# An attention and gMLP kernel on one core: the output product of batches five and six as seven block products

## The chip, the core and the metric

The kernel runs on one core of a Trainium2 chip. Its time is the device time of one execution in microseconds (us), given as the median of several runs. Names of engines here: TensorE (PE in rows, PEld where it loads weights), VectorE (DVE), ScalarE (ACT), GpSimd (POOL), and SyncE (SP), which here issues every DMA.

## What is computed

The input is q, k and v for 8 batches of 8 heads with 576 positions of 64 channels, and the weights of one gated layer. All of it is float32.

```
q_s = softmax(q, over the 64 channels);  k_s = softmax(k, over the 576 positions)
x   = heads joined( q_s @ (k_s^T @ v) )                 # per batch 576 x 512
h   = gelu(x @ w_in)                                     # 512 -> 1024
u, v = the two halves of h
v_n = layernorm(v) * g_ln
v_s = w_sg @ v_n + b_sg                                  # 576 x 576 over positions
out = x + (u * v_s) @ w_out                              # 512 -> 512
```

The last line's product is the one that is changed, in two of the eight batches.

## The kernel before

Batches are numbered 0 to 7. Everything of a batch lies with channels on the 128 partitions and the 576 positions along a row, so that a 512-channel matrix is four row blocks of 128. Each large product is made in float32 precision from three products of a reduced format: an operand z is stored as a high part (a cast, on ScalarE) and a low part (z minus its high part, on VectorE or GpSimd), and high*high, high*low and low*high are summed in PSUM.

The steps of a batch, by the names that stand in the code:

- `kv_all` multiplies exp(k) with v, and `x_mm` multiplies that by q; `x_kv` (L708) issues both, `x_mm` of one batch and `kv_all` of the next. `x_get` and `x_tail` (ScalarE) copy x from PSUM to `xf`, of which there are two, for even and odd batches.
- `hv_mm` makes the v half of h, 128 positions at a time (12 matmuls of 512 columns); `hv_gelu`, `hv_sq` or `hv_stat`, `hv_norm`, `hv_high` and `hv_low` follow, and leave the normed v in the two tiles `vnh` and `vnl`.
- The u half of h is computed from batch 2 on by seven block products, as Strassen's method in Winograd's form has it: `us_mm` 1 to 7 (L913), 12 matmuls of 128x288 each, on sums of blocks of x (`d_add`, `d_high`, `d_low`) and of w_in (the `sw_` steps, made once). `us_one` and `us_add` (L945) gather the blocks from three PSUM tiles, `us_gelu` follows.
- `sg_mm` is the product with w_sg, 28 matmuls of 128x288 for each of four 128-channel blocks d; `gate` multiplies by u in place, `gate_high` (L975) and `gate_low` (L978) split the product.
- `out_mm` (L990) is the output product: for each of four blocks e of 128 output channels 24 matmuls of 128x288 (four blocks d, three pairs of parts, two column halves). `out_add` (L993) adds it to x in `xf` on VectorE, `out_store` (L997) writes 288 KB to memory. In the last batch the fourth block goes by `last_mm`, in three pieces.

PSUM has three tiles of two banks (`ps2`), which products take in rotation, and two of one bank (`ps1`) for `hv_mm` and `kv_all`. The order of all work is a string of step names, PLAN, that is read once from front to back: each engine's queue, and SyncE's queue of DMAs, is in the order in which PLAN names the steps, and an engine runs its own queue strictly in that order. Semaphores between engines follow from which tile a step reads and writes; a tile with a tag of its own has a fixed home in SBUF, and a new tile in the same home waits until all users of the one before are through.

All matmuls are issued by the helper at L246, all work of the other engines by the helper at L160 of the class InOrder, so in the profile lines tell little and tiles tell what a row is.

Of the kernel before, what the change touches and what calls it, by code (L numbers as in the profile page):

```python
# [51 lines left out]
hv_norm 0 0, load_kt 2 2, q_mul 1 1 0, q_turn 1 2, kv_mm 1 0, kv_inv 1 0, hv_stat 0 0 A, kv_scale 1 0, kv_mm 1 1, kv_inv 1 1, load_w_sg 0, ws_h 0
hv_sq 0 2, hv_stat 0 2 A, kv_scale 1 1, load_q 2 0, load_kt 2 3, kt_max 2 3, x_mm 1, x_get 1 1, kt_max 2 2, load_q 2 1, ws_l 0, x_tail 1, q_max 2 0
hv_pow 0 2, load_v 2 0, hv_pow 0 0, load_b, x_endh 1, load_kt 3 0, hv_norm 0 3, x_sum 1, x_endl 1, hv_norm 0 2, load_w_sg 4, x_get 1 0, hv_mm 0 1
x_high 1 0, x_low 1 0, x_high 1 1, x_low 1 1, hv_gelu 0 1, hv_pow 0 3, hv_high 0 3, hv_low 0 3, hv_high 0 2, hv_low 0 2, hv_high 0 0, hv_stat 0 1
hv_mm 0 4, load_k 2 0, hv_norm 0 1, hv_pow 0 1, x_ownh 1, kt_put 2, ws_h 4 V, hv_gelu 0 4, hv_stat 0 4, hv_mm 1 1, hv_gelu 1 1 A, hv_sq 1 1
hv_high 0 1, load_v 2 1, hv_norm 0 4, hv_low 0 1, ws_l 2 V, hv_low 0 0, hv_mm 1 0, q_max 2 1, hv_pow 0 4, kt_max 3 0, tail_high 0, tail_low 0
tail_again 0, b_h, b_l, ws_l 4 V, hv_gelu 1 0 A, hv_mm 1 3, sg_mm 0 1, tail_high 1, load_w_out 0, load_k 2 1, kt_get 2, wo_a 0, hv_sq 1 0, sg_mm 0 0
k_sub 2 0, load_kt 3 2, hv_gelu 1 3, q_swapm 2 0, k_sub 2 1, wo_b 2, k_exp 2 0, load_kt 3 1, k_exp 2 1, wo_b 0, wo_d 2, q_swapm 2 1 G, q_top 2 1
wo_h 2, wo_d 0, wo_h 0, sg_mm 0 3, gate 0 0, gate_high 0 0, gate 0 1, hv_mm 1 2, gate_high 0 1, kt_max 3 1, q_sub 2 1, kt_max 3 2, tail_low 1  # L60
q_top 2 0, wo_l 0 V, q_sub 2 0, gate 0 3, load_kt 3 3, kt_max 3 3, kt_put 3, kt_get 3, q_exp 2 1, q_sum 2 1, sg_mm 0 2, wo_l 2 V, hv_gelu 1 2 A
hv_sq 1 2, kv_all 2, gate 0 2, q_exp 2 0, gate_high 0 2, load_k 3 1, q_swapd 2 1, load_k 3 0, gate_low 0 0, gate_high 0 3, gate_low 0 1, gate_low 0 2
gate_low 0 3 G, hv_stat 1 0 A, q_sum 2 0, q_inv 2 1, load_v 3 0, kv_inv 2 0, kv_scale 2 0, out_mm 0 0, out_add 0 0, kv_inv 2 1, q_swapd 2 0 G
q_inv 2 0, kv_scale 2 1, hv_stat 1 3, q_mul 2 0 0 V, q_mul 2 1 1, tail_again 1, q_turn 2 3, out_mm 0 3, out_add 0 3, q_mul 2 0 1, q_turn 2 1
q_mul 2 1 0, q_turn 2 2, k_sub 3 1 G, k_exp 3 1, q_turn 2 0, out_mm 0 1, load_kt 4 0, out_add 0 1, load_v 3 1, k_sub 3 0, out_mm 0 2, out_add 0 2
x_ownl 1, out_store 0 1, sw_get 1 1, k_exp 3 0, x_kv 2, hv_norm 1 1, hv_stat 1 1 A, out_store 0 0, x_get 2 0, hv_norm 1 3, sw_get 1 0, out_store 0 2
sw_add 1, sw_high 1, out_store 0 3, kt_max 4 0, x_tail 2, x_get 2 1, sw_get 0 0, hv_pow 1 3, hu_mm 1 2, sw_add 3, hu_gelu 1 2, hv_stat 1 2 A, sw_add 2
sw_high 2, hu_mm 1 0, hu_gelu 1 0, load_kt 4 1, kt_max 4 1, hu_mm 1 3, kv_inv 3 0, kv_scale 3 0, hv_pow 1 0, hv_pow 1 1, hv_high 1 1, kv_inv 3 1
sw_get 0 1, sw_add 4, load_k 4 1, kv_scale 3 1, sw_low 1, load_v 4 0, load_kt 4 2, kt_max 4 2, load_kt 4 3, kt_max 4 3, kt_put 4, hv_norm 1 0
hv_high 1 0, hv_norm 1 2, hv_low 1 0, sw_high 3, hv_pow 1 2, hv_low 1 1, hv_high 1 2, sw_low 2, sw_low 3, load_kt 5 0, kt_get 4, hv_high 1 3  # L70
hv_low 1 2, sw_high 4, sw_low 4, hv_low 1 3, load_q 3 0, hu_gelu 1 3, kt_max 5 0, hu_mm 1 1, x_high 2 0, x_high 2 1, sg_mm 1 0, q_max 3 0, q_swapm 3 0
# [1014 lines left out]
```

## Time and profile before

| | |
|---|---|
| median of 3 runs | 481.65 us (481.62, 481.65, 483.18) |
| the profiled execution's own time | 482.25 us |
| its span, first to last instruction | 480.4 us |
| TensorE busy | 474.9 us (99%) |
| TensorE loading weights | 437.7 us (91%) |
| VectorE busy | 372.8 us (78%) |
| ScalarE busy | 272.8 us (57%) |
| GpSimd busy | 141.8 us (30%) |

The busy time of TensorE is modelled, since its matmuls overlap each other: one matmul of 128x288 lasts 0.29 us in a row, and the next one begins after 0.13 us. The pace is therefore read from the times at which matmuls start. The granted clock of TensorE is 1.00 in every stretch that is shown, which is the level of 2.4 GHz. The rows that matter stand below, ahead of the prediction.

### The profile page before, as it was taken

To read this page: it belongs to the slowest core of one execution; us is meant where nothing else is said; L and a number is where in the kernel's file an instruction comes from. 1 tells how busy PE (TensorE), PEld (TensorE's weight loads), DVE (VectorE), ACT (ScalarE), POOL (GpSimd) and SP (SyncE) were. 2 spreads that over 40 slices of the span, in tenths; PEclk is the share of its full clock that TensorE was granted. 3 is DMA by queue.
4 is the path that set the end of the run, shared out by engine and by line. 5 is a ranking of instruction groups with operands and counts; after the bars stand their busy time and mean duration, and the time that the engine had idled before them with its cause. 6 is when DMAs were issued, how large, how long until landed. Compare 5 with 4: busy or idle time off the path is not lost.

```text
span 480.4 us, 9342 instructions
## 1 busy us (share of the span) xinstructions
PE 474.9 (99%) x3813; PEld 437.7 (91%) x3813; DVE 372.8 (78%) x604; ACT 272.8 (57%) x439; POOL 141.8 (30%) x157
## 2 busy tenths in 40 slices
...
GB/s 307 367 407 200 297 187 69 192 210 191 242 47 53 124 175 138 49 155 159 154 0 1 157 144 89 132 26 124 51 1 27 75 0 1 1 0 76 0 1 124
DMA packets 20637, 57.11 MB, mean 119 GB/s; under 512 B 3057, under 2 KB 3569, under 8 KB 20594
## 3 DMA queue, kind: packets, MB, share of 16 engines
...
## 4 chain that ended last, share of the span: by engine, by line
PE 90%; DVE 4%; ACT 2%; DMA 2%; issue 1%; POOL 0%; POOLq 0%
PE ps L246 90%; DMA qq<-q 1%; DMA kmt<-kt 1%; DVE xf L160 1%; DVE qqw L160 1%; DVE wi_l L160 0%; ACT qs L160 0%; DVE ktall L160 0%; DVE v L160 0%; ACT qq L160 0%; ACT vnh L160 0%; DVE qm L160 0%; ACT x_l L160 0%; ACT xf L160 0%; DVE wi_h L160 0%
## 5 line engine op out<-in xcount | busy, mean ns | idle before, releaser
L160 DVE TENSOR_TENSOR u<-ps,u 128x576 f32<-128x576 f32 x62 | 46.3, 753 | 35.7 <-PE ps L246 32.9
L160 POOL TENSOR_TENSOR rs<-ve,half 128x1 f32<-128x1 f32 x36 | 27.8, 779 | 116.3 <-DVE ve L160 115.2
L246 PE MATMUL ps<-gh,wo_h 128*128 128x288 f32 (+1 forms) x260 | 56.5, 295 | 0.0
L246 PE MATMUL ps<-gh,wo_l 128*128 128x288 f32 (+1 forms) x260 | 56.2, 293 | 0.0
L246 PE MATMUL ps<-ws_h,vnh 128*128 128x288 f32 x256 | 55.0, 296 | 0.4 <-ACT u L160 0.4
L246 PE MATMUL ps<-ws_l,vnh 128*128 128x288 f32 x256 | 54.8, 295 | 0.0
L246 PE MATMUL ps<-ws_h,vnl 128*128 128x288 f32 x256 | 54.8, 295 | 0.0
L160 ACT ACTIVATE v<-ps 128x512 f32<-128x512 f32 x36 | 21.4, 596 | 39.3 <-PE ps L246 39.0
L160 ACT ACT_TABLE_LOAD x30 | 38.5, 1283 | 8.4 <-PE ps L246 4.0
L246 PEld LDWEIGHTS ps<-gh,wo_h 128*128 128x128 f32 x260 | 42.3, 189 | 0.7
L246 PEld LDWEIGHTS ps<-ws_h,vnh 128*128 128x128 f32 x256 | 41.5, 188 | 1.1 <-ACT u L160 0.6
L246 PEld LDWEIGHTS ps<-gh,wo_l 128*128 128x128 f32 x260 | 42.2, 188 | 0.0
L246 PEld LDWEIGHTS ps<-ws_l,vnh 128*128 128x128 f32 x256 | 41.3, 188 | 0.0
L246 PEld LDWEIGHTS ps<-ws_h,vnl 128*128 128x128 f32 x256 | 41.3, 188 | 0.0
L246 PE MATMUL ps<-wi_l,x_h 128*128 128x512 f32 x144 | 39.6, 396 | 0.2 <-DVE wi_l L160 0.2
L246 PE MATMUL ps<-wi_h,x_h 128*128 128x512 f32 x144 | 39.6, 397 | 0.1
L160 DVE TENSOR_TENSOR xf<-ps,xf 128x576 f32<-128x576 f32 (+2 forms) x34 | 24.0, 714 | 20.2 <-PE ps L246 20.1
L246 PE MATMUL ps<-wi_h,x_l 128*128 128x512 f32 x144 | 39.6, 396 | 0.0
L160 ACT CAST gh<-u 128x576 fp32r<-128x576 f32 x32 | 21.0, 670 | 25.5 <-DVE u L160 24.8
L246 PEld LDWEIGHTS ps<-wi_l,x_h 128*128 128x128 f32 x144 | 27.0, 188 | 7.1 <-DVE wi_l L160 0.6
L246 PEld LDWEIGHTS ps<-wi_h,x_l 128*128 128x128 f32 x144 | 27.0, 188 | 6.9 <-DVE x_l L160 0.5
L160 ACT ACTIVATE vnh<-v,rs 128x512 fp32r<-128x512 f32 x32 | 22.2, 719 | 17.5 <-DVE v L160 13.8
...
## 6 DMA issues: line engine op xcount, KB each, us to landing
...
out<-xf SPq DMA_DIRECT2D x31, 288.0 KB, 2.1
...
kmt<-kt SPq DMA_DIRECT2D x24, 288.0 KB, 3.0
...
ghws<-w_sg SPq DMA_DIRECT2D x5, 288.0 KB, 8.2
```

Of the source, the lines that this page charges most:

```text
L160: ins = op(*args, **kw)
L246: tc.keep_in_program_order(nc.tensor.matmul(*args, **kw))
```

## The change

In batches 5 and 6 (`SEVEN = range(5, B - 1)`) the steps `out_mm`, `out_add` and `out_store` are gone. In their place stand seven block products `os_mm` 1 to 7 of 12 matmuls each, on 2x2 blocks of the gated product (128 x 2 x 288) and of w_out (128 x 2 x 256).

- Once: `so_get` (4) adds high and low parts of a block of w_out, `so_add` (4) makes the four sums that the method needs, `so_high` and `so_low` (4 each) split them. They lie in the homes of k (`kk`), v (`vv`) and the transposed k (`km`), which are free once batch 7 has used them.
- For each of the two batches: `e_add` (4) makes sums of blocks of the gated product in place, `e_high` and `e_low` (4 each) split them, into `vnh` and `vnl` and a half of the first gated tile; nine `os_add` gather the result from three PSUM tiles into `xf`; four `os_store` write it. Of the first two blocks d `gate_high` and `gate_low` split only the first 288 columns there, and the low part of the last two lies in a home of v.
- From `hv_gelu 0 3` on, PLAN is a new string: the same steps otherwise, in another order, in batches 0 to 7.

The diff without PLAN:

```diff
+SEVEN = range(5, B - 1)
...
     def gate_rest(b, d):
         if d < 2:
-            return sd_all()[:, 12 * DH + d * S:12 * DH + d * S + S]
+            return low_one()[:, d]
+        if b in SEVEN:
+            return vv_s("low", b, at=1, shape=[P, 2, S], dt=F32R)[:, d - 2]
         return uu_s("low", b, at=0, dt=F32R)[:, d - 2]
+    def used(b, d):
+        return slice(0, HS if b in SEVEN and d < 2 else S)
...
+    def o_block(i, j):
+        hi, lo = wo_hl()
+        return block(hi, i, j, DH), block(lo, i, j, DH)
+
+    def o_parts(n):
+        if n == 3:
+            return [km_s("so", t, at=1 - t, dt=F32R)[:, 0:2 * DH].rearrange("p (c n) -> p c n", c=2) for t in range(2)]
+        z = (vv_s if n == 4 else kk_s)("so", n, at=n - 1 if n < 3 else 0, shape=[P, 2, 2, DH], dt=F32R)
+        return [z[:, t] for t in range(2)]
...
+    def so_get(i, j, E=V):
+        hi, lo = o_block(i, j)
+        E.tensor_tensor(out=o_whole(i, j), in0=f32(hi), in1=f32(lo), op=ALU.add)
...
+        a, b, op = {
+            1: (o_whole(1, 0), o_whole(1, 1), ALU.add), 2: (o_whole(1, 1), o_whole(0, 0), ALU.subtract),
+            3: (o_whole(0, 0), o_whole(1, 0), ALU.subtract), 4: (o_whole(0, 1), o_whole(1, 1), ALU.subtract),
+        }[n]
...
+    def e_parts(b, n):
+        if n == 1:
+            return [gh_s(b, 0, at=0)[:, :, HS:S], low_one()[:, :, HS:S]]
+        k, z = 2 * n - 4, [y.rearrange("p a n -> p (a n)") for y in vn_hl()]
+        return [z[m // 3][:, m % 3 * S:m % 3 * S + S].rearrange("p (c n) -> p c n", c=2) for m in (k, k + 1)]
+
+    def e_sum(b, n):
+        return u_block(b, *{1: (0, 0), 2: (1, 1), 3: (0, 1), 4: (1, 0)}[n])
+
+    def e_add(b, n, E=V):
+        x, y = {1: ((0, 1), (0, 0)), 3: ((1, 1), (0, 1)), 2: ((1, 1), (0, 0)), 4: ((1, 0), (1, 1))}[n]
+        E.tensor_tensor(out=e_sum(b, n), in0=u_block(b, *x), in1=u_block(b, *y), op=ALU.subtract)
...
+    def os_mm(b, n, fresh=0):
+        l, r, name = {
+            1: (o_block(0, 0), lambda: g_block(b, 0, 0), "oa"), 2: (o_block(0, 1), lambda: g_block(b, 1, 0), "oa"),
+            3: (o_parts(4), lambda: g_block(b, 1, 1), "oc"), 4: (o_block(1, 1), lambda: e_parts(b, 4), "ob"),
+            5: (o_parts(1), lambda: e_parts(b, 1), "oc"), 6: (o_parts(2), lambda: e_parts(b, 2), "ob"),
+            7: (o_parts(3), lambda: e_parts(b, 3), "ob"),
+        }[n]
...
+        for s in range(2):
+            fs, m = slice(s * P, s * P + P), 0
+            for p, q in ((0, 0), (1, 0), (0, 1)):
+                for c in range(2):
+                    mm(st[name, b][:, s, 0:HS], l[p][:, c, fs], r[q][:, c], start=bool(fresh) and m == 0, stop=m == 5, skip_group_check=not fresh)
+                    m += 1
...
+    def os_add(b, k, i, j):
+        o = xf(b)[:, 2 * i:2 * i + 2, j * HS:j * HS + HS]
+        V.tensor_tensor(out=o, in0=us_sum(b, banks[k]), in1=o, op=ALU.add)
+
+    def os_store(b, i, j):
+        js = slice(j * HS, j * HS + HS)
+        to = out[b, 2 * i * P:(2 * i + 2) * P, js].rearrange("(c p) n -> p c n", c=2)
+        Y.dma_start(out=to, in_=xf(b)[:, 2 * i:2 * i + 2, js])
```

What the new order does is shown at three places, in the queues of the engines. The helpers' lines are L160 and L246 before, L166 and L252 after; the digits in a tile's name are the batch and the block, and a number of the allocation.

**First place: ScalarE's queue in batch 1.** Here `u1_..<-ps2` is `hu_gelu 1` (the gelu of one 128-channel block of u, which frees a PSUM tile), and `qs3_0<-qm3_0` is `q_swapm 3 0`, which waits for a maximum over a q tile that a DMA has to bring. Before:

```order
L160 ACTIVATE u1_1_1378<-ps2_0_80 128x576
L160 CAST x_h_74<-xf0_76 128x2x576 x2
L160 COPY qs3_0_1548<-qm3_0_1546 32x36 x4
L160 ACTIVATE u1_0_1408<-ps2_1_81 128x576
L160 ACT_TABLE_LOAD
```

and with the change:

```order
L166 ACTIVATE u1_0_1371<-ps2_0_80 128x576
L166 CAST wi_h_61<-qqw_1_1279 128x2x256
L166 CAST x_h_74<-xf0_76 128x2x576
L166 CAST sd_1112<-qqw_1_1279 128x512
L166 ACTIVATE u1_1_1428<-ps2_1_81 128x576
L166 COPY qs3_0_1583<-qm3_0_1576 32x36 x4
```

The last gelu of batch 1's u stands ahead of the copies that wait for the q tile; before it stood behind them.

**Second place: ScalarE's queue behind `x_kv 6`.** `xf0<-ps2` are `x_get 6 0`, `x_get 6 1` and (128x2x2x64) `x_tail 6`; `ghd` are high parts for `us_mm`; `u5_1<-ps2` is `us_one 5`. Before:

```order
L160 CAST ghd_5_2_3746<-ud_5_0_3722 128x576
L160 CAST sd_1117<-ud_5_1_3604 128x576
L160 COPY xf0_76<-ps2_1_81 128x2x512
L160 COPY xf0_76<-ps2_2_82 128x2x512
L160 ACTIVATE vnh_607<-v5_0_3554,rs5_0_3689 128x512
L160 COPY xf0_76<-ps2_0_80 128x2x2x64
L160 COPY u5_1_3868<-ps2_1_81 128x2x288
```

and with the change, where `kkso_1` is `so_high 1`, whose home is that of batch 7's k:

```order
L166 ACTIVATE vnh_586<-v5_2_3506,rs5_2_3596 128x512
L166 ACTIVATE vnh_586<-v5_3_3626,rs5_3_3672 128x512
L166 COPY xf0_76<-ps2_1_81 128x2x512
L166 CAST kkso_1_3849<-kmso_1_1_3541 128x512
L166 CAST ghd_5_2_3859<-ud_5_0_3757 128x576
L166 COPY xf0_76<-ps2_2_82 128x2x512
L166 CAST ghd_5_4_3867<-ud_5_0_3757 128x576
L166 COPY u5_1_3881<-ps2_1_81 128x2x288
L166 COPY xf0_76<-ps2_2_82 128x2x2x64
```

Two splits and a cast of a w_out sum now stand between the three copies that free PSUM; the cast waits for the last read of k by `kv_all 7`.

**Third place: TensorE's queue at the end of batch 5's output product.** `gh5`, `ulow_5` are the gated product's parts, `wo_h` and `wo_l` those of w_out, `vnh`, `vnl` here the parts of the e sums, `qt7` and `kvt7` the operands of `x_mm 7`. Before, the end of `out_mm 5 2`, `hv_mm 6 2`, and the start of `x_mm 7`:

```order
L246 MATMUL ps2_2_82<-gh5_1_4083,wo_l_961 128x288 x2
L246 MATMUL ps1_1_84<-wi_h_61,x_h_74 128x512 x4
L246 MATMUL ps1_1_84<-wi_h_61,x_l_75 128x512 x4
L246 MATMUL ps1_1_84<-wi_l_62,x_h_74 128x512 x4
L246 MATMUL ps2_0_80<-qt7_0_4137,kvt7_0_4014 64x512
```

and with the change, the end of `os_mm 5 2`, `os_mm 5 4`, and `x_mm 7`:

```order
L252 MATMUL ps2_2_82<-vvlow_5_4168,wo_h_951 128x288 x2
L252 MATMUL ps2_0_80<-vnl_587,wo_h_951 128x288 x2
L252 MATMUL ps2_0_80<-vnl_587,wo_l_952 128x288 x2
L252 MATMUL ps2_0_80<-vnl_587,wo_h_951 128x288 x4
L252 MATMUL ps2_0_80<-vnl_587,wo_l_952 128x288 x2
L252 MATMUL ps2_0_80<-vnl_587,wo_h_951 128x288 x2
L252 MATMUL ps2_2_82<-qt7_0_4028,kvt7_0_4106 64x512
L252 MATMUL ps2_2_82<-qt7_0_4028,kvt7_1_4095 64x512
L252 MATMUL ps2_2_82<-qt7_0_4028,kvt7_0_4106 64x512
L252 MATMUL ps2_2_82<-qt7_0_4028,kvt7_1_4095 64x512
L252 MATMUL ps2_0_80<-qt7_1_4171,kvt7_0_4106 64x512
```

No `hv_mm` stands between the output product and `x_mm 7` any more, and the second half of `x_mm 7` takes the PSUM tile `ps2_0` that the last block product has just filled. The three `hv_mm` of batch 6 (for positions 0, 3 and 2 of the blocks of 128) stand ahead of `os_mm 5 6` instead.

## Rows read from the trace of the kernel before

**Rows 1.** The page: span, and busy time of each engine.

```profile
span 480.4 us, 9342 instructions
PE 474.9 (99%) x3813; PEld 437.7 (91%) x3813; DVE 372.8 (78%) x604; ACT 272.8 (57%) x439; POOL 141.8 (30%) x157
```

**Rows 2.** Chain that ended last: start us, us, what; its last long pieces, from a DMA on.

```profile
119.21 5.02 DMA qq<-q
...
126.57 0.66 ACT u L160
...
127.27 350.32 PE ps L246 x2720
```

**Rows 3.** TensorE's timeline: start us, us of the merged row, shapes, count, idle before.

```profile
71.76 1.04 PE L246 MATMUL ps<-ws,vn 128*128 128x288 f32 x4
...
126.19 0.70 PE L246 MATMUL ps<-ws,vn 128*128 128x288 f32 x4
127.27 0.53 PE L246 MATMUL ps<-ws_h,vnh 128*128 128x288 f32 x2 [0.38 <-ACT u L160]
```

**Rows 4.** TensorE's timeline at an output product: an `out_mm`, an `hv_mm`, the next `out_mm`.

```profile
309.73 0.43 PE L246 MATMUL ps<-gh,wo_h 128*128 128x288 f32 x2
...
312.89 1.09 PE L246 MATMUL ps<-wi_h,x_h 128*128 128x512 f32 x4
...
315.68 0.43 PE L246 MATMUL ps<-gh,wo_h 128*128 128x288 f32 x2
```

**Rows 5.** TensorE's timeline from `x_mm` and `kv_all` on to block products `us_mm`.

```profile
328.10 2.18 PE L246 MATMUL ps<-qt,kvt 64*64 64x512 f32 x32
330.10 2.43 PE L246 MATMUL ps<-vv,kk 64*64 64x65 f32 x80
332.46 0.53 PE L246 MATMUL ps<-x_h,wi_h 128*128 128x288 f32 x2
...
334.17 1.75 PE L246 MATMUL ps<-ghd,sd 128*128 128x288 f32 x12
335.75 1.76 PE L246 MATMUL ps<-sd 128*128 128x288 f32 x12
```

**Rows 6.** Costliest groups by form: shapes, count | busy us, mean ns | idle before, releaser.

```profile
L160 DVE TENSOR_TENSOR xf<-ps,xf 128x576 f32<-128x576 f32 x31 | 23.0, 748 | 14.8 <-PE ps L246 14.8
L160 ACT COPY xf<-ps 128x1024 f32<-128x1024 f32 x14 | 13.9, 1016 | 4.3 <-PE ps L246 2.4 <-DMA out<-xf 1.9
L160 DVE TENSOR_TENSOR qqw<-wi_h,wi_l 128x512 f32<-128x512 f32 x4 | 2.7, 680 | 0.0
L160 ACT CAST sd<-qqw 128x512 fp32r<-128x512 f32 x3 | 1.8, 611 | 2.4 <-DVE qqw L160 2.4
L160 ACT CAST sd<-ud 128x576 fp32r<-128x576 f32 x6 | 4.0, 670 | 1.3 <-PE ps L246 1.3
```

**Rows 7.** VectorE's timeline: two splits of the same form, one behind the other.

```profile
329.39 0.76 DVE L160 TENSOR_TENSOR ghd<-ud,ghd 128x576 fp32r<-128x576 f32 x1 [0.92 <-ACT ghd L160]
330.07 0.76 DVE L160 TENSOR_TENSOR sd<-ud,sd 128x576 fp32r<-128x576 f32 x1
```

**Rows 8.** Stretches: from:to, us; busy (x) of PE, PEld, DVE, ACT, POOL; clock, DMA.

```profile
60.00:120.00 60.00, 59.89 (x552) 55.77 (x551) 57.10 (x97) 40.57 (x67) 28.89 (x22) 1.00 0.52 170
271.24:328.58 57.34, 57.34 (x469) 53.11 (x464) 46.03 (x74) 33.22 (x49) 9.32 (x16) 1.00 0.33 107
328.58:380.34 51.76, 51.76 (x445) 48.63 (x440) 37.91 (x62) 26.52 (x48) 11.73 (x13) 1.00 0.13 46
```

**Rows 9.** DMA issues: KB each, median us to landing; then least, median, longest.

```profile
out<-xf SPq DMA_DIRECT2D x31, 288.0 KB, 2.1
DMA to landing us min/median/max: 1.6/2.1/5.0
```

**Rows 10.** The tile `sd`: splits on VectorE and GpSimd, ns least/median/longest.

```profile
L160 DVE TENSOR_TENSOR sd<-u,gh x9: 749/753/1368, 87.6 to 460.8; 128x576 fp32r<-128x576 f32 x9
L160 POOL TENSOR_TENSOR sd<-u,gh x7: 1422/1435/2267, 141.6 to 461.7; 128x576 fp32r<-128x576 f32 x7
```

More of the change, by code (lines that the diff above doesn't have):

```diff
@@ L52 @@
[L52 to L71, printed above, removed]
@@ new lines @@
+so_low 1, out_store 4 2, d_add 5 4, d_high 5 2, x_get 6 1, so_get 0 0, kv_inv 7 0, d_low 5 2, d_high 5 4, us_mm 5 1, us_one 5, so_add 2, d_low 5 4
+x_tail 6, x_high 6 0, so_add 3, us_mm 5 5, us_add 5 5, q_inv 7 0, hv_pow 5 1, us_mm 5 6, so_get 0 1, us_add 5 6, hv_high 5 0, hv_low 5 0, hv_high 5 1
+hv_low 5 1, hv_low 5 3, us_mm 5 2, us_gelu 5 0 0, kv_inv 7 1, hv_low 5 2, so_high 2, us_mm 5 3, us_add 5 3, us_mm 5 7, x_high 6 1, sg_mm 5 1
+us_add 5 7, us_gelu 5 1 1, so_add 4, x_low 6 1, load_q 7 1, q_max 7 1, q_mul 7 0 0, us_gelu 5 0 1, q_mul 7 0 1 V, q_swapm 7 1, q_top 7 1, us_mm 5 4
@@ new lines @@
+us_add 5 4, q_turn 7 0, sg_mm 5 0, gate 5 1, x_low 6 0, gate 5 0, so_low 2, us_gelu 5 1 0, gate_high 5 1, sg_mm 5 3, q_sub 7 1, q_exp 7 1
+kv_scale 7 1, gate_high 5 0, gate_low 5 0 G, q_sum 7 1, q_swapd 7 1, kv_scale 7 0, gate_low 5 1, e_add 5 1, so_high 3, so_low 3, gate 5 3, sg_mm 5 2
+gate 5 2, q_inv 7 1, q_mul 7 1 0, os_mm 5 1, os_add 5 0 1 1, e_high 5 1, os_add 5 0 0 1, gate_high 5 2, so_high 4, so_low 4, gate_high 5 3
+gate_low 5 3, gate_low 5 2 G, q_turn 7 2, hv_mm 6 0, hv_gelu 6 0, hv_mm 6 3, hv_mm 6 2, e_add 5 3, e_add 5 2, e_high 5 2, os_add 5 0 1 0, e_low 5 2
```

202 lines of the change are left out of this document (126 added, 76 removed).

## The prediction

> **What bounds the kernel now.** First the page's busy shares: TensorE is busy 99% of the span, VectorE 78%, ScalarE 57%, GpSimd 30% [rows 1]. The reader is to see that one engine alone can hold the end, but not yet that it does. So next the chain that ended last: its final long piece is TensorE from 127.27 us on, 350.32 us without a break; ahead of it stands a DMA of q and ScalarE's gelu of u [rows 2]. Then TensorE's own timeline. In the chain's last 350 us no wait is named; of the waits ahead of that, after the 42 us in which both kernels have one order, two count. At 126.19 four matmuls start and the next row only at 127.27, 1.08 us later, where four take 0.53 us at the pace found below: 0.55 us lost to ScalarE's `u`. At 71.76 the row of four lasts 1.04 us, the same four at 126.19 0.70: another 0.34 us [rows 3]. Together **0.9 us** of waits in the old order; all else of that stretch is issue pace.
>
> The pace is in the starts. The 24 matmuls of `out_mm` begin at 309.73 and the next work at 312.89: 3.16 us, 0.132 us each; the 12 of `hv_mm` behind them take 315.68 - 312.89 = 2.79 us [rows 4]. The block products that the kernel already has (`us_mm`, the same shape, loop and operand types as `os_mm`) start 335.75 - 334.17 = 1.58 us apart for 12, again 0.132 us each [rows 5]. So a block product costs TensorE what its matmul count says and nothing else.
>
> **The change, part by part.** The sum is made against the profiled execution: 482.25 us, of which 480.4 is span [rows 1] and 1.85 lies around it. It stands 0.60 us above the median of the runs shown, 481.65.
>
> *Matmuls.* Four `out_mm` of 24 are 96 matmuls, seven `os_mm` of 12 are 84. Two batches: 24 fewer, 3813 to 3789 in the page's count [rows 1]. At 3.16 us for 24 [rows 4] the saving is **-3.16 us**, all on the path, since TensorE runs without a break there. The Trainium skill, "TensorE: Matmul & The Clock Gate", § Back-to-back issue gap, gives for a stream of weight loads and matmuls 81 ns at 128 columns and 131 ns at 512; between them 288 columns would take 102 ns, and the 24 an estimate of 2.4 us. The rows differ: 132 ns at 288 columns and, by `hv_mm`, 2.79 / 12 = 233 ns at 512.
>
> *The new order.* The first place shows the last gelu of batch 1's u ahead of the copies that wait for a q tile. The q tile's DMA took 5.02 us and that gelu ended the wait at 127 us [rows 2], so this wait should go. Where else the new order waits no row shows. Bounds: all 0.9 us of the old waits go and none comes (-0.9); or the old ones stay and as much again comes (+0.9). I take half, **-0.45 us**, nearest to the one wait of 0.55 whose cause is seen to be moved [rows 3].
>
> *The last place of the order.* `x_mm 7` now follows `os_mm 5 4` directly, and its second half fills the PSUM tile that `os_mm 5 4` has just ended in. It must wait for one `os_add`, a DVE addition from PSUM of 0.75 us [rows 6], behind the last matmul, 0.43 - 0.13 = 0.30 us [rows 4]: 1.05 us. Its cover is the first half of `x_mm`, half of 330.10 - 328.10 = 2.00 us [rows 5]. So 0 to 0.15 us: I take **+0.1**.
>
> *Work off TensorE.* Once: 4 `so_get` and 4 `so_add`, 0.68 us like `qqw` [rows 6], 4 `so_low`, 0.68 (two splits start 330.07 - 329.39 apart) [rows 7]. Per batch: 4 `e_add` and 4 `e_low`, again 0.68, and nine `os_add` of 128x2x288 for four `out_add` of 128x576, the same count of elements and 0.75 us in a row [rows 6], 0.68 in start distance. In all 12 + 16 + 10 = 38 more operations, some 25 us of VectorE. ScalarE gets 4 `so_high` at 0.61 and 8 `e_high` at 0.67 [rows 6], 7.8 us, less about 1.3 for gates that now split half a row. I cost all of it at nothing, and the cover is the idle time of these engines. By stretch: from `x_mm 5` to `x_mm 6` VectorE was busy 46.03 of 57.34 us, from there to `x_mm 7` 37.91 of 51.76 [rows 8]. Counted by steps in the changed queue, 19 operations worth 15.6 us come into the first and 9 worth 7.3 go: 54.3 of 57.3 us, 95%. In the second 30 worth 22.3 come and 16 worth 13.9 go: 46.3 of 50.2 us (12 matmuls shorter), 92%. Nothing lies there that a stretch of this kernel has not carried: 57.10 of 60 us, 95%, at 60 to 120 us, where TensorE still lost only the 0.34 us at 72 [rows 3, 8]. The rest falls behind `x_mm 7`, where VectorE has most room.
>
> *Waits that the change adds.* `so_high 1` takes the home of batch 7's k, so ScalarE stops until `kv_all 7` has read it; `kv_all` ends 332.46 - 328.10 = 4.4 us behind `x_mm`'s start [rows 5]. Queued behind it on ScalarE are two splits and a copy of `x_get`; the copy takes 1.02 us [rows 6], and TensorE, which fills that PSUM tile again as its next but two, has by my count 0.4 to 1.0 us to spare. Nothing added, but it is the tightest place there. The first `os_mm` of batch 5 that reads an e sum has three `hv_mm` ahead of it, 8.4 us [rows 4]; in batch 6 `os_mm 6 1`, two `hv_mm` and `os_mm 6 5`, 1.58 + 5.58 + 1.58 = 8.7 us [rows 4, 5]. The stores keep size and count, 288 KB and four a batch; their landing took 2.1 us in the median and 5.0 at most [rows 9], and only the copies of `x_get 7` into `xf` wait for them. Nothing again.
>
> **Sum:** 482.25 - 3.16 - 0.45 + 0.1 = 478.74 for an execution like the profiled one, 0.7% less; on the median of 481.65 that is **478.1 us**. About 0.5%, 2.4 us, is what a measurement of this kernel can tell from no change.
>
> **Rivals.** *A. VectorE becomes the bound in the two stretches.* First the rows: splits on VectorE took 753 ns in the median and up to 1368, 0.61 us more, and GpSimd's own 1435 and up to 2267 [rows 10]: the long ones fall on each other. The change adds 28 VectorE operations with two operands in SBUF, and seven long GpSimd operations remain in the two stretches by my count of its queue. Seven collisions are 7 x 0.61 = 4.3 us, where VectorE's idle time is 57.3 - 54.3 = 3.0 us in the first stretch and the densest row kept 2.9 of 60 idle [rows 8]. So in the first there is no room, and in the second about 1.5 us above that floor: 4.3 - 0.3 - 1.5 = 2.5 us given back, 478.1 + 2.5 = **480.6**. For it: the 95%. Against it: such collisions are already in the 57.10 of 60 that cost nothing. The Trainium skill, "SBUF — State Buffer", § Who interferes with whom, states this as a lock on the pair of ports that VectorE shares with GpSimd; the trace agrees by the 1368 ns. Chance 0.17.
>
> *B. The matmul count is not what TensorE is bound by.* Its weight loads fill 91% of the span [rows 1], so each matmul would have slack of its own and fewer of them would only lengthen pauses: no gain, **481.6**. Against it: the starts are evenly 0.132 us apart in two unlike products [rows 4, 5], and pauses would be uneven. The Trainium skill, "Perfetto Trace Analysis", § Identifying the Most-Contended Engine, judges TensorE by the busy share of weight loads and not by that of matmuls; by that 9% would be free, and the even starts are against it. Chance 0.03.
>
> *C. The e sums come too late (slower).* The place is the first `os_mm` on an e sum, in each of the two batches. Behind the last matmul of `sg_mm` comes a chain: 0.30 for that matmul [rows 4], 0.75 for the gate (priced as the other PSUM-fed DVE operation), 0.75 for `e_add`, 0.67 for `e_high` [rows 6], 0.76 for `e_low` [rows 7]: 3.2 us, in which TensorE stands if nothing covers it. Twice, 6.4 us: 478.1 + 6.4 = **484.5**, +0.6%. It decides from the point at which VectorE or ScalarE run 8.4 - 3.2 = 5.2 us behind at that place. For it: both engines stand in strict order, and `so_high 1` can hold ScalarE up. Against it: 8.4 us of cover and 4 us of idle VectorE in that stretch. Chance 0.08.
>
> *D. The order does not do what it says:* the 127-us wait is replaced by others of 2 us in the reordered batches 0 to 4, some 480.5. Chance 0.04.
>
> **How the numbers follow.** The forecast's case has 0.68. Its own range follows from the bounds: -3.16 - 0.9 to -3.16 + 0.9 + 0.15, which is 477.6 to 479.5 on the median; run-to-run spread takes the low end to 477.2. Rivals A, B and D lie at 480.5 to 481.6; to leave no more than 2 in 10 outside, the range goes to 480.8. **Range 477.2 to 480.8.** Faster means under 479.24: nearly all of the forecast's case and a few of A: 0.69. Within 0.5%, to 484.06: A, B, D and the case's upper edge: 0.22. Slower: C and a little of A at its worst: 0.09.
>
> **What would show it.** Right: 3789 matmuls; 12 of `os_mm` in 1.58 us; no wait on ScalarE's `u` near 127 us; `x_mm 7` with at most 0.15 us between its halves; VectorE at about 95 and 92% in the two stretches, and TensorE's last chain piece still unbroken. Wrong: TensorE's waits on VectorE or ScalarE adding up to over 1.2 us, splits over 1 us in number between `x_mm 5` and `x_mm 7` (A), a pace of `os_mm` above 0.132 (B), or a gap ahead of the first `os_mm` on an e sum (C).

## The result, and the profile after

The changed kernel takes **478.18 us** (median of 4 runs, 477.85 to 478.41), the kernel before 482.13 (4 runs, 481.62 to 483.18). The ratio is 0.9915 with a 95% interval of 0.9895 to 0.9935: 0.85% faster, beyond the 0.5% that counts as a change. The prediction was 478.1.

The page of the changed kernel, the rows that answer to [rows 1]:

```profile
span 476.2 us, 9353 instructions
PE 471.3 (99%) x3789; PEld 434.6 (91%) x3789; DVE 396.1 (83%) x642; ACT 281.6 (59%) x453; POOL 139.9 (29%) x157
```

TensorE has 24 matmuls less and is still busy 99%; VectorE has 38 operations and 23.3 us more. The span is shorter by 480.4 - 476.2 = 4.2 us. The end of its chain of waits (start us, us, what), against [rows 2]:

```profile
37.56 28.12 PE ps L252 x232
...
65.69 407.78 PE ps L252 x3272
...
473.49 0.31 DVE xf L166
```

The last unbroken piece of TensorE begins at 65.69 us, no longer at 127.27: the wait on ScalarE's `u` is gone, and behind 65.69 us none has come; what ends at 65.69 is looked at under "The order" below. TensorE's timeline (start us, us, what, count) shows it at that place and at the block products of batch 5:

```profile
125.87 0.70 PE L252 MATMUL ps<-ws,vn 128*128 128x288 f32 x4
126.41 0.43 PE L252 MATMUL ps<-ws_h,vnh 128*128 128x288 f32 x2
...
366.56 1.09 PE L252 MATMUL ps<-wi_l,x_h 128*128 128x512 f32 x4
367.49 1.76 PE L252 MATMUL ps<-vnh,kkso 128*128 128x288 f32 x12
369.09 0.70 PE L252 MATMUL ps<-gh,kkso 128*128 128x288 f32 x4
...
377.16 2.24 PE L252 MATMUL ps<-qt,kvt 64*64 64x512 f32 x32
```

The next row now starts 126.41 - 125.87 = 0.54 us behind four matmuls, where it was 1.08 [rows 3]. The 12 matmuls of `os_mm 5 6` are followed 369.09 - 367.49 = 1.60 us later by the next block product, 0.133 us each. `x_mm 7` lasts 2.24 us, 0.06 more than `x_mm 6` in [rows 5].

Where the 4.2 us come from (4.12 before the two spans are rounded) is read from one `x_mm` to the next (from:to, us; busy of PE, PEld, DVE, ACT, POOL; clock, DMA, GB/s). The mark of an `x_mm` lies 0.48 us behind its first matmul, in every kernel alike. First the kernel before, from `x_mm 2` to `x_mm 6` and from `x_mm 7` to the last matmul (the stretch between is in [rows 8]):

```profile
102.48:328.58 226.10, 225.72 (x1849) 209.77 (x1844) 183.09 (x289) 134.96 (x209) 72.96 (x86) 1.00 0.36 117
380.34:477.58 97.24, 97.24 (x700) 92.94 (x692) 54.81 (x90) 32.68 (x53) 10.64 (x11) 1.00 0.06 23
```

The same of the changed kernel, with the stretch from `x_mm 5` to `x_mm 6` apart:

```profile
102.17:327.38 225.21, 225.21 (x1848) 209.59 (x1844) 188.92 (x302) 141.77 (x218) 72.44 (x90) 1.00 0.35 117
...
270.12:327.38 57.26, 57.26 (x468) 53.07 (x464) 49.35 (x79) 35.54 (x54) 8.96 (x13) 1.00 0.24 88
327.38:377.64 50.26, 50.26 (x433) 47.22 (x428) 46.49 (x75) 27.17 (x48) 9.19 (x10) 1.00 0.10 33
377.64:473.46 95.82, 95.82 (x688) 91.37 (x680) 63.99 (x104) 34.75 (x57) 11.74 (x12) 1.00 0.08 29
```

So 0.31 us by `x_mm 2`, 0.89 from there to `x_mm 6`, 51.76 - 50.26 = 1.50 with batch 5's seven products, 97.24 - 95.82 = 1.42 with batch 6's: 4.12 in all, and the tail behind the last matmul is the same. In each of these stretches of the changed kernel TensorE is busy throughout.

That looks as if there had been room for all of it. VectorE's timeline around the e sums of batch 5 says otherwise:

```profile
359.30 1.42 DVE L166 TENSOR_TENSOR xf<-ps,xf 128x576 f32<-128x576 f32 x2 [0.34 <-PE ps L252]
360.63 0.68 DVE L166 TENSOR_TENSOR vvso<-vvso,vvso 128x512 fp32r<-128x512 f32 x1
361.42 2.02 DVE L166 TENSOR_TENSOR vvlow<-u,gh 128x576 fp32r<-128x576 f32 x1
363.37 0.77 DVE L166 STREAM_TRANSPOSE qt<-qq 128x576 f32<-128x576 f32 x1
364.06 1.57 DVE L166 TENSOR_TENSOR u<-u,u 128x576 f32<-128x576 f32 x2
365.55 0.75 DVE L166 TENSOR_TENSOR xf<-ps,xf 128x576 f32<-128x576 f32 x1
366.38 0.76 DVE L166 TENSOR_TENSOR vnh<-u,vnh 128x576 fp32r<-128x576 f32 x1
...
369.72 0.75 DVE L166 TENSOR_TENSOR xf<-ps,xf 128x576 f32<-128x576 f32 x1
```

From 359.30 to 375.31 there is no idle time above 0.11 us. `u<-u,u` are the e sums, `vnh<-u,vnh` is `e_low 5 2`, which ends at 367.14, 0.35 us ahead of `os_mm 5 6` (its first four matmuls need the high part alone, 4 x 0.133 us, so some 0.9 us are to spare). The last row is `os_add 5 1 0 1`. It ends at 370.47 and has to read its PSUM tile before `os_mm 5 7` adds to it, which starts 1.59 us behind `os_mm 5 5`, at 369.09 + 1.59 = 370.68: **0.2 us to spare**. The 2.02 us of `gate_low 5 3` fall on GpSimd's split of the same tile:

```profile
361.40 1.43 POOL L166 TENSOR_TENSOR vvlow<-u,gh 128x576 fp32r<-128x576 f32 x1 [1.20 <-DVE vvso L166]
```

Three questions follow. How is the gain shared between the products and the order? Is VectorE's queue at the e sums the next limit, and what does the collision with GpSimd do there? Where would a further cut of TensorE's work end?

### The profile page after: what moved, and what is told of

Its sections match the earlier page's. It is cut to its first block, busy times and chain, and to the rows that moved or that the text cites. A ratio compares the mean times of both kernels' runs of the same rounds, so it can differ in the third digit from the quotient of the medians.

```text
span 476.2 us, 9353 instructions
## 1 busy us (share of the span) xinstructions
PE 471.3 (99%) x3789; PEld 434.6 (91%) x3789; DVE 396.1 (83%) x642; ACT 281.6 (59%) x453; POOL 139.9 (29%) x157
## 4 chain that ended last, share of the span: by engine, by line
PE 96%; ACT 2%; DVE 1%; issue 1%; POOL 0%; POOLq 0%
PE ps L252 96%; DVE xf L166 1%; DVE wi_l L166 0%; ACT qq L166 0%; ACT qs L166 0%; ACT x_l L166 0%; ACT xf L166 0%; DVE wi_h L166 0%; ACT kk L166 0%; POOL vn L166 0%; ACT x_h L166 0%; DVE kr L166 0%; DVE kvt L166 0%; POOLq L1183 0%
## 5 line engine op out<-in xcount | busy, mean ns | idle before, releaser
L166 DVE TENSOR_TENSOR u<-ps,u 128x576 f32<-128x576 f32 x62 | 46.2, 753 | 26.8 <-PE ps L252 26.2
L166 POOL TENSOR_TENSOR rs<-ve,half 128x1 f32<-128x1 f32 x36 | 27.4, 770 | 129.4 <-DVE ve L166 128.1
L252 PE MATMUL ps<-ws_h,vnh 128*128 128x288 f32 x256 | 54.9, 296 | 0.0
L252 PE MATMUL ps<-ws_l,vnh 128*128 128x288 f32 x256 | 54.9, 296 | 0.0
L252 PE MATMUL ps<-ws_h,vnl 128*128 128x288 f32 x256 | 54.8, 296 | 0.0
L252 PE MATMUL ps<-gh,wo_l 128*128 128x288 f32 (+1 forms) x212 | 46.1, 294 | 0.0
L252 PE MATMUL ps<-gh,wo_h 128*128 128x288 f32 (+1 forms) x212 | 46.0, 294 | 0.0
L166 DVE TENSOR_TENSOR xf<-ps,xf 128x576 f32<-128x576 f32 (+2 forms) x44 | 31.3, 723 | 14.4 <-PE ps L252 14.1
L166 ACT CAST gh<-u 128x576 fp32r<-128x576 f32 (+1 forms) x34 | 21.5, 643 | 36.4 <-DVE u L166 36.3
L252 PEld LDWEIGHTS ps<-ws_h,vnh 128*128 128x128 f32 x256 | 41.6, 189 | 0.5
L252 PEld LDWEIGHTS ps<-ws_h,vnl 128*128 128x128 f32 x256 | 41.3, 189 | 0.0
L252 PEld LDWEIGHTS ps<-ws_l,vnh 128*128 128x128 f32 x256 | 41.3, 188 | 0.0
L252 PE MATMUL ps<-wi_h,x_h 128*128 128x512 f32 x144 | 39.9, 398 | 0.1
L252 PE MATMUL ps<-wi_l,x_h 128*128 128x512 f32 x144 | 39.6, 396 | 0.2 <-DVE wi_l L166 0.2
L252 PE MATMUL ps<-wi_h,x_l 128*128 128x512 f32 x144 | 39.4, 396 | 0.0
L166 ACT ACTIVATE v<-ps 128x512 f32<-128x512 f32 x36 | 21.4, 597 | 23.6 <-PE ps L252 22.3
L252 PEld LDWEIGHTS ps<-gh,wo_h 128*128 128x128 f32 x212 | 34.5, 188 | 0.4
L252 PEld LDWEIGHTS ps<-gh,wo_l 128*128 128x128 f32 x212 | 34.4, 188 | 0.0
L252 PEld LDWEIGHTS ps<-wi_l,x_h 128*128 128x128 f32 x144 | 27.0, 188 | 7.0 <-DVE wi_l L166 0.6
L252 PEld LDWEIGHTS ps<-wi_h,x_l 128*128 128x128 f32 x144 | 27.0, 188 | 6.5
L166 POOL TENSOR_TENSOR qq<-qq,qd 128x576 f32<-128x576 f32 (+2 forms) x18 | 22.5, 1260 | 30.0 <-DVE qd L166 14.6
```

What stands on the lines that cost most here:

```text
L166: ins = op(*args, **kw)
L252: tc.keep_in_program_order(nc.tensor.matmul(*args, **kw))
```

## The experiments

**The products of before, in the new order.** First in the whole new order:

```diff
-SEVEN = range(5, B - 1)
+SEVEN = ()
...
-os_mm 5 2, os_add 5 0 0 0, q_turn 7 3, os_mm 5 4, os_add 5 1 1 0, hv_stat 6 0, x_kv 7
+q_turn 7 3, out_mm 5 2, out_add 5 2, out_store 5 2, hv_stat 6 0, x_kv 7
```

Four of the seven `os_mm` of each batch become an `out_mm` with its `out_add` and `out_store` in this way, and all other steps that the change has added are gone.

> The new order with the output products of before: batches 5 and 6 by out_mm again (24 matmuls more, no e sums, no sums of w_out), everything else in the changed kernel's order. Theory (the 24 matmuls are worth their pace, the order the rest): span 476.2 + 2.9 to 3.2 = 479.1 to 479.4 us, and about 481.3 in the median, 0.9 to 1.2 below before. Rival (the order is worth nothing, the whole gain is the products'): span 480.4, 482.1. Second rival (the order is worth more and the products cost something): span below 478.5.

Measured: 488.6 us, ratio 1.0122 (1.0102 to 1.0142). None of the cases. Up to `x_mm 7` it is as the theory has it (51.73 us from 327.24); behind it stand waits of my own making. TensorE and ScalarE, rows of their timelines, then two stretches, from `x_mm 7` to the last matmul and a part of it:

```profile
388.54 0.54 PE L269 MATMUL ps<-x_h,wi_h 128*128 128x288 f32 x2 [3.59 <-ACT xf L183]
...
389.63 0.68 PE L269 MATMUL ps<-x_h,wi_h 128*128 128x288 f32 x2
390.11 0.68 PE L269 MATMUL ps<-x_h,wi_l 128*128 128x288 f32 x2
```

```profile
386.20 0.37 ACT L183 COPY xf<-ps 128x256 f32<-128x256 f32 x1 [5.84 <-DMA out<-xf]
```

```profile
378.97:484.33 105.36, 100.36 (x700) 94.56 (x692) 58.23 (x95) 33.89 (x55) 12.46 (x12) 0.98 0.07 24
389.19:392.52 3.33, 3.33 (x14) 3.04 (x13) 2.52 (x4) 3.08 (x6) 0.00 (x0) 0.50 0.00 0
```

The copy of x of batch 7 waits for the store of batch 5 to leave `xf`, since I had put the last `out_mm 5` and its store directly ahead of `x_kv 7`. In the changed kernel `os_mm 5 4` stands at that place, but an `os_store` writes one half of the positions, and the copy that comes first, that of the last 64, needs only the two stores of the second half; an `out_store` writes all positions of a block, so here it needs all four. TensorE stands idle for 105.36 - 100.36 = 5.0 us of this stretch (1.2 of them in batch 7, waiting for VectorE's `u`), and its own work takes 100.36 us instead of 97.24: behind the 3.59 us of idle time the granted clock was 0.50, the level of 1.2 GHz, from 389.2 to 392.6 us, where matmuls of 288 columns start 0.24 us apart. The second try takes the new order up to `x_kv 6` alone, and that of before from there on:

```diff
-x_kv 6, x_get 6 0, hv_stat 5 3, x_get 6 1, d_low 5 3, hv_high 5 0, us_mm 5 1, hv_stat 5 1
+x_kv 6, x_get 6 0, out_store 4 2, d_add 5 4, d_high 5 2, x_get 6 1, d_low 5 2, hv_high 5 0, us_mm 5 1
```

Ahead of this line stands the change's order without `so_get` and `so_add`, behind it that of before without the steps that are done by then.

> The kernel before with the changed kernel's order up to x_kv 6 (without the steps for sums of w_out) and its own order behind it: the reorder of batches 0 to 5 alone, all products as before. The first try at this (the changed order throughout, with out_mm) showed x_mm 6 at 327.24 us and then waits of its own of 3.8 and 1.3 us for stores that I had put late. Theory (the order's gain is made by x_mm 6 and nothing is lost behind it): x_mm 6 at 327.2 to 327.5 instead of 328.6, span 479.1 to 479.4, median about 481.0. Rival (the order only borrows, and the stretch behind pays back): span 480.0 or more.

Measured: 481.03 us (12 runs), ratio 0.9969 (0.9959 to 0.998). Its stretches, as above:

```profile
102.08:327.29 225.21, 225.21 (x1848) 209.53 (x1844) 188.00 (x299) 141.79 (x218) 71.45 (x89) 1.00 0.37 117
327.29:379.01 51.72, 51.72 (x444) 48.58 (x440) 32.18 (x54) 23.37 (x41) 10.22 (x11) 1.00 0.12 41
379.01:476.30 97.29, 97.28 (x700) 92.98 (x692) 54.81 (x90) 32.73 (x53) 10.61 (x11) 1.00 0.06 23
```

The first stretch is that of the changed kernel to the hundredth, the other two are those of before to 0.05 us. So in the profiled executions the order is worth 0.89 us behind `x_mm 2`, and the seven products 51.72 - 50.26 = 1.46 and 97.29 - 95.82 = 1.47 us. The theory holds. Whole runs add one thing: the 12 of this kernel take 480.85 to 481.38 us, the 22 of before beside them 481.38 to 483.88. The old order varies more, and what makes it vary no trace here shows.

**One gelu moved.** The kernel before, with the step that the first place of the change shows:

```diff
-q_max 3 0, q_swapm 3 0, x_low 2 1, x_low 2 0, load_q 3 1, sg_mm 1 2, k_sub 4 1 G, hu_gelu 1 1, q_top 3 0
+q_max 3 0, hu_gelu 1 1, q_swapm 3 0, x_low 2 1, x_low 2 0, load_q 3 1, sg_mm 1 2, k_sub 4 1 G, q_top 3 0
```

> The kernel before with one step moved: the last gelu of batch 1's u (hu_gelu 1 1) ahead of the copies that wait for the q tile (q_swapm 3 0). Theory (that wait was 0.55 us of the old order's 0.9): no wait of TensorE on ScalarE's u near 127 us, span 480.4 - 0.55 = 479.8. Rival (the wait is handed on, to the next PSUM tile or to the gates of batch 1): the wait turns up within 5 us under another name, span 480.2 to 480.5.

Measured: 481.4 us, ratio 0.9989 (0.9973 to 1.0005); span 479.4. The time alone can't tell it from before, the trace can. TensorE's timeline, and the stretch from `x_mm 2` to `x_mm 6`:

```profile
125.63 0.70 PE L268 MATMUL ps<-ws,vn 128*128 128x288 f32 x4
126.17 0.43 PE L268 MATMUL ps<-ws_h,vnh 128*128 128x288 f32 x2
...
179.03 0.43 PE L268 MATMUL ps<-ws_l,vnh 128*128 128x288 f32 x2
179.43 0.80 PE L268 MATMUL ps<-ws,vn 128*128 128x288 f32 x4
```

```profile
101.88:327.65 225.77, 225.77 (x1849) 209.83 (x1844) 183.65 (x289) 134.99 (x209) 73.52 (x86) 1.00 0.36 117
```

The wait at 126 us is gone, but 0.24 us come back at 179 us (0.40 us between two rows that stand 0.27 apart before, and a row of four that lasts 0.80 instead of 0.70). Of 0.55 us, 226.10 - 225.77 = 0.33 stay. Cut at `x_mm 3`, the stretch before is 56.83 and 169.27 us, here 56.23 and 169.54, in the changed kernel 56.13 and 169.08: the moved gelu is worth 0.60 us (the wait and slower starts behind it), the second wait costs 0.27, and the rest of the new order gives another 0.10 and 0.19 us. Whether the moved gelu brings that second wait is open: a wait of 0.25 us near there, at 184 us, stands in one of the eight traces with the changed kernel's queue and in no other. And the mark of `x_mm 2` lies at 101.88, 0.60 earlier than in the profiled execution of before, with the same queue up to there: the first 100 us differ between executions, and this mark lies anywhere from 101.88 to 102.57 us in the traces of this case. The 0.31 us that the changed kernel gained there say nothing of the order.

**Less cover.** One `hv_mm` of batch 6 goes from ahead of `os_mm 5 6` to behind `os_mm 5 4`, with its gelu:

```diff
-hv_mm 6 0, hv_gelu 6 0, hv_mm 6 3, hv_mm 6 2, e_add 5 3
+hv_mm 6 0, hv_gelu 6 0, hv_mm 6 3, e_add 5 3
...
-q_mul 7 1 1 V, hv_stat 6 3 A, hv_gelu 6 2, os_add 5 2 0 1
+q_mul 7 1 1 V, hv_stat 6 3 A, os_add 5 2 0 1
...
-os_mm 5 4, os_add 5 1 1 0, hv_stat 6 0
+os_mm 5 4, hv_mm 6 2, os_add 5 1 1 0, hv_gelu 6 2, hv_stat 6 0
```

> The changed kernel with hv_mm 6 2 (2.79 us) behind os_mm 5 4 instead of ahead of os_mm 5 6, so that the e sums of batch 5 have one product less as cover. In the changed kernel's trace the second split of the e sums ends at 367.13 us and os_mm 5 6 starts at 367.49: 0.36 us to spare. Theory (the cover is used up to those 0.36 us): TensorE waits 2.79 - 0.36 = 2.4 us ahead of os_mm 5 6 and gets nothing back, span 476.2 + 2.4 = 478.6. Rival (the prediction's estimate, cover 5.2 us longer than the chain needs): no wait, span 476.1 to 476.3. In between, if VectorE's work catches up: 0.5 to 2.

Measured: 480.89 us, 2.7 more than the changed kernel. TensorE's timeline, then its stretch from `x_mm 6` to `x_mm 7`:

```profile
366.80 2.13 PE L274 MATMUL ps<-vnh,kkso 128*128 128x288 f32 x12 [1.54 <-ACT vnh L188]
368.76 0.69 PE L274 MATMUL ps<-gh,kkso 128*128 128x288 f32 x4
...
371.02 0.77 PE L274 MATMUL ps<-vnh,kmso 128*128 128x288 f32 x4 [0.51 <-DVE xf L188]
```

```profile
327.79:380.84 53.05, 51.00 (x433) 47.07 (x429) 49.13 (x80) 27.03 (x48) 9.21 (x10) 1.00 0.12 40
```

53.05 - 50.26 = 2.79 us: as much as the moved product lasts, a little over the theory's 2.4 and over the 2.79 - 0.2 = 2.6 that the addition's 0.2 us to spare would leave. Slower starts behind the two waits make up the rest. The wait falls in two, on ScalarE's high part of e 2 (which waits for VectorE's sum) and, as the 0.2 us to spare had it, on `os_add` ahead of `os_mm 5 7`. The cover that the prediction called 5.2 us too long was used up to 0.2.

**Three VectorE operations more, at two places.** The same count, once ahead of the e sums and once where VectorE stands idle:

```diff
-so_low 4
+so_low 4, so_low 4, so_low 4, so_low 4
```

```diff
-d_low 7 2
+d_low 7 2, d_low 7 2, d_low 7 2, d_low 7 2
```

> The changed kernel with three repeats of so_low 4 (VectorE, 128x512, about 0.61 us each, 1.83 in all) directly behind it, ahead of batch 5's e sums. Theory (VectorE runs without idle time from there to the e sums, 0.36 us to spare): TensorE waits about 1.5 us ahead of os_mm 5 6, span 477.7. Rival (busy shares decide: the stretch has 50.26 - 46.49 = 3.77 us of idle VectorE, which takes 1.83): span 476.2.

> The changed kernel with three repeats of d_low 7 2 (VectorE, 0.67 us each, 2.0 us in all) where VectorE stands idle for 2.28 us ahead of 430.84 us; the counterpart of the three repeats ahead of the e sums of batch 5, which cost 1.48 us between x_mm 6 and x_mm 7. Theory (the place decides): no new wait, from x_mm 7 to the last matmul 95.8 us as in the changed kernel, span 476.2, 0.4 more or less for the first 100 us. Rival (any added VectorE work costs): 1 us or more.

Measured: 479.57 us for the first, 477.95 for the second. The first one's stretch from `x_mm 6` to `x_mm 7`, and the second one's from `x_mm 7` to the last matmul:

```profile
327.38:379.12 51.74, 51.01 (x433) 47.19 (x428) 47.87 (x78) 27.16 (x48) 9.77 (x10) 1.00 0.10 32
```

```profile
377.57:473.38 95.81, 95.81 (x688) 91.38 (x680) 66.16 (x107) 34.75 (x57) 11.74 (x12) 1.00 0.08 29
```

1.48 us against nothing (95.82 in the changed kernel). The first stretch had 50.26 - 46.49 = 3.77 us of idle VectorE, and three short operations still cost 1.48 of their 1.83 us: most of the idle part lies ahead of the place, none at it.

**Less cover, and GpSimd's split on VectorE.** One edit more on the kernel with less cover:

```diff
-gate_low 5 2 G
+gate_low 5 2
```

> The kernel with hv_mm 6 2 behind os_mm 5 4 again (53.05 us from x_mm 6 to x_mm 7, 2.79 more than in the changed kernel), with one more edit: gate_low 5 2 on VectorE instead of GpSimd. On GpSimd it ran beside VectorE's gate_low 5 3, which took 2.02 us instead of 0.75, and the e sum behind it 0.15 longer. Theory (VectorE's own queue sets the wait, and the shared work with GpSimd lengthens that queue): VectorE gains 1.27 + 0.15 and gets 0.68 more, the wait shrinks by 0.7, 52.3 us from x_mm 6 to x_mm 7, span 478.7. Rival (the 2.02 us is no contention and gate_low costs VectorE its full time on top): 53.7 us, span 480.1.

Measured: 480.26 us, 0.6 less than with GpSimd. VectorE's row of the two splits, and the stretch from `x_mm 6` to `x_mm 7`:

```profile
361.80 1.43 DVE L188 TENSOR_TENSOR vvlow<-u,gh 128x576 fp32r<-128x576 f32 x2
```

```profile
327.76:380.14 52.38, 51.00 (x432) 47.06 (x428) 48.53 (x81) 27.04 (x48) 7.76 (x9) 1.00 0.12 41
```

Two splits on VectorE take 1.43 us, where one took 2.02 beside GpSimd: handing one to GpSimd made VectorE later. The stretch is 53.05 - 52.38 = 0.67 us shorter, as expected.

**A further cut of TensorE's work.** Each `os_mm` leaves out the low parts of w_out and its sums:

```diff
-            for p, q in ((0, 0), (1, 0), (0, 1)):
+            for p, q in ((0, 0), (0, 1)):
```

> The changed kernel with each block product of the output made from two of its three pairs of parts, without the low parts of w_out and its sums times the high parts: 28 matmuls less in each of batches 5 and 6, 3.73 us each, all other engines' work as it was. It asks what holds the end once TensorE is faster there. Theory (in batch 5 VectorE is the next bound, almost at once: no idle time from 359.6 to 374.7 us): from x_mm 6 to x_mm 7 about 49 us instead of 50.26, 1.3 saved of 3.7; in batch 6, where VectorE has idle time, 3 or more of 3.7; span 471 to 472. Rival (TensorE alone holds the end): 46.5 us in that stretch, span 468.8.

Measured: 474.21 us, span 472.5. Its stretches, and its waits of TensorE (releaser: us in total, times, longest):

```profile
327.46:375.97 48.51, 47.06 (x404) 43.57 (x400) 45.62 (x74) 27.16 (x48) 9.19 (x10) 1.00 0.08 28
375.97:469.67 93.70, 92.73 (x660) 87.73 (x652) 64.26 (x105) 34.63 (x57) 11.74 (x12) 1.00 0.09 32
```

```profile
PE ps L274 <- DVE xf L188: 1.7, 3, 0.9
...
PE ps L274 <- DVE vnl L188: 0.7, 1, 0.7
```

Up to the mark of `x_mm 7` it saves 50.26 - 48.51 = 1.75 of 3.73 us, behind it 95.82 - 93.70 = 2.12. But the second half of `x_mm 7`, behind the mark, waits for batch 5's last addition, 0.4 us with its slower starts; with these put to batch 5, that batch saves 1.3, as expected, and batch 6 2.5, where I had expected 3 or more. TensorE now waits for VectorE's additions in batch 5 and for a split in batch 6. So the changed kernel stands close to where the two engines change places, in both batches.

**The last batch by seven products too.**

```diff
-SEVEN = range(5, B - 1)
+SEVEN = range(5, B)
...
-sg_mm 7 3, gate 7 3, gate_high 7 3, gate_low 7 3, out_mm 7 2
+sg_mm 7 3, e_add 7 1, e_high 7 1, gate 7 3, gate_high 7 3, e_low 7 1, os_mm 7 1, os_mm 7 5, e_add 7 3, gate_low 7 3
...
```

This is the second try's order; the steps of the seven products follow in both, in place of `out_mm 7` and `last_mm 7`. The first try takes one low part from a block that an e sum has already overwritten, so it does not compute this product and only its time is of use; in the second the last addition and store go in two halves.

> The changed kernel with the last batch's output product by seven block products too: 84 matmuls of 128x288 in place of the equal of 96 (1.6 us less TensorE), 3 e sums more on VectorE and nine additions for the tail, no product of a next batch as cover, and the end of the kernel right behind it. Theory (without cover VectorE holds the end): behind the last sg_mm VectorE has some 17 operations of 0.68 us, 11.6 us, beside 11.2 us of TensorE, and they wait for each other; TensorE waits 1 to 2 us in all, the last store is larger (288 KB, 2.1 us, instead of 72 KB, 1.6): span 475.5 to 477, no gain that can be measured. Rival (the 12 matmuls count as in batches 5 and 6): span 474.7 or less.

> The last batch by seven block products again, in a better order. In the first try (477.7 us) the low part of the fourth gated block was taken after an e sum had overwritten it, so its output was not the reference's; TensorE waited 1.2 us ahead of os_mm 7 6 and 0.4 us each ahead of 7 2 and 7 4, and the span ended 4.05 us behind its last matmul, 2.79 in the changed kernel. Now the gate of block 3 stands ahead of the split of e 1, that low part ahead of e 2, and the last addition and store go in two halves. Theory (behind the last sg_mm, without a product as cover, VectorE's 17 operations set the end): waits of 1 to 2 us stay, the tail is 3.2 to 3.5 us, span 475.4 to 476.4, the median within 0.8 us of the changed kernel's. Rival (the first try was only badly ordered, and the 12 matmuls count in full): span 474.7 or less, median under 476.8.

Measured: 479.42 us for the first try, 478.18 for the second (4 runs, 478.14 to 478.26), the changed kernel's own time. The second one's wait ahead of `os_mm 7 6`, and its stretch from `x_mm 7` to the last matmul:

```profile
464.11 2.12 PE L276 MATMUL ps<-vnh,kkso 128*128 128x288 f32 x12 [1.23 <-ACT vnh L190]
```

```profile
377.65:472.67 95.02, 93.79 (x664) 88.81 (x656) 71.64 (x115) 36.87 (x61) 11.11 (x12) 1.00 0.07 23
```

TensorE ends 95.82 - 95.02 = 0.8 us earlier instead of 1.5, and the span of 476.4 ends 476.4 - 472.67 = 3.7 us behind the last matmul, where the changed kernel needs 2.8, since a larger addition and store come last. Without the next batch's products as cover the method pays nothing here: neither version beats the changed kernel.

## Why the prediction was right, point by point

**Matmuls.** Forecast -3.16 us, measured -1.46 and -1.47, together -2.93 (the order held fixed); 0.06 us of a longer `x_mm 7`, below, are in it, so the matmuls alone gave -2.99. The term was 0.17 us too large: the 168 matmuls of `os_mm` go at 0.133 us, not at the 0.132 of `out_mm`. (The prediction's sign for rival B, a pace above 0.132, was drawn too fine: it came, by 0.001.) Rival B, by which fewer matmuls bring no gain, falls by the same numbers. They do not tell the pace of the matmuls from that of their weight loads, since each matmul brings one of its own: both counts fell from 3813 to 3789, and the loads stayed at 91% of the span. The Trainium skill, "Perfetto Trace Analysis", § Identifying the Most-Contended Engine, judges TensorE by the share of its peak arithmetic rate and by the busy share of weight loads. By the second 9% would be free; whether anything could use it no run here shows.

**The order.** Forecast -0.45 within -0.9 to +0.9, measured -0.89 behind `x_mm 2`: the lower bound. The wait at 127 us went as forecast, and the moved gelu alone gave 0.60 us there in its one trace; the other 0.29 us are tied to no wait. The 0.34 us at 72 us were a wait of the old order: the row of four lasts 1.04 and 0.93 us in the two traces with the old queue, 0.7 in the ten with the new one. But the new order has a wait of about that size in its place, at 65 us, in all ten. TensorE before, then TensorE and its weight loads with the change:

```profile
64.79 1.10 PE L246 MATMUL ps<-wi_l,x_h 128*128 128x512 f32 x4
65.73 1.10 PE L246 MATMUL ps<-wi_h,x_h 128*128 128x512 f32 x4
```

```profile
64.59 1.09 PE L252 MATMUL ps<-wi_l,x_h 128*128 128x512 f32 x4
65.69 1.20 PE L252 MATMUL ps<-wi_h,x_h 128*128 128x512 f32 x4
...
65.69 0.76 PEld L252 LDWEIGHTS ps<-wi_h,x_h 128*128 128x128 f32 x4 [0.45 <-ACT ps L166]
```

From row to row it is 65.69 - 64.59 = 1.10 us where it was 65.73 - 64.79 = 0.94, and the row behind is 0.1 us longer; the weight load waits for ScalarE. So the old wait at 72 us and the new one at 65 us about cancel, and the new order has brought a wait of 0.3 us where rival D feared 2. The 0.31 us by which the changed kernel was ahead at `x_mm 2` lie within the 0.6 us by which the first 100 us vary between executions of one queue.

**The last place of the order.** Forecast 0.1, measured 0.06 in the row of `x_mm 7`.

The terms were off by +0.17, -0.44 and -0.04 us, so they partly took each other back: with the measured terms the sum gives 478.43 for the profiled execution, where 478.74 was forecast and 478.29 measured. What is left is the first 100 us and the time around the span. That the median came within 0.1 us of the forecast's 478.1 is luck: the forecast stands on a median of before of 481.65 from three runs, and the sets of runs of before beside the experiments have medians of 481.82 to 482.62. On the 482.13 of the result the same sum would have given 478.6.

**Work off TensorE, at nothing.** Right in its sum (23.3 us of VectorE against 25 forecast, 8.8 of ScalarE against 6.5, with two table loads of 1.28 us that the forecast left out) and in its cost, wrong in the reason. In the first stretch VectorE stands at 49.35 of 57.26 us, 86%, not at 95: I counted the steps that the queue names between two `x_mm`, and VectorE need not do them there. Before, it spent 3.0 us behind `x_mm 5` (272.07 to 275.07) on steps that the queue names ahead of it; in the changed kernel it is through with all such steps by then. In the second the forecast was 92% and 92% it is, but the 3.8 us that are left do not lie where they are wanted.

**The e sums (rival C).** This is the step that failed. "It decides from the point at which VectorE or ScalarE run 8.4 - 3.2 = 5.2 us behind": the chain of five operations was priced right, but VectorE's queue holds nine others between the gate and `e_low 5 2` (two parts of a softmax, three additions from PSUM, a split of w_out's sums, a split of the gate that takes 2.02 us, a transpose, the sum of e 3), and the nearest wait was not on the chain at all but on an addition that frees a PSUM tile. To spare were 0.2 us. The forecast came true, and its chance of 0.08 for this rival was set by a margin over twenty times too wide. Most of that stands in the queue itself: thirteen VectorE operations lie between 359.30 us and that addition, and at the 0.68 us of [rows 7] each they and its own 0.75 end at 368.9, an estimate, 1.8 us ahead of the 370.68. Most of the rest went to the collision with GpSimd.

**Contention (rival A).** Shown, and off the path by that same small margin. Between `x_mm 5` and `x_mm 7` VectorE has one split above 1 us, where the rival counted seven collisions; at that place the collision lengthened VectorE's queue by 2.02 - 0.75 = 1.3 us, and undoing it took 0.67 us from a kernel without spare cover. The Trainium skill, "SBUF — State Buffer", § Who interferes with whom, states the lock of the shared ports; the 2.02 us against 0.75 agree. In the changed kernel itself it costs nothing.
